# Four tiles of scores in plain fp32 from 40 rows of q and k, and a reordered start

## The chip, the cores and the metric

The kernel runs on one core of a Trainium2 chip. The metric is the device time of one execution in microseconds (us), the median of three timed runs. The core's engines work side by side, each through its own queue in order: TensorE (PE, matrix products), VectorE (DVE), ScalarE (ACT), GpSimd (POOL) and SyncE (SP), which here issues every DMA. An engine that waits for data holds up everything behind it in its queue.

## The reference, cut to what matters

Three parts run one behind another, all in fp32. The first is a gated recurrence (mLSTM) over 2 batches, 8 heads, 768 steps and head size 40:

```python
m_new  = np.maximum(f_gate[t] + m, i_gate[t])
f_stab = np.exp(f_gate[t] + m - m_new); i_stab = np.exp(i_gate[t] - m_new)
C = f_stab * C + i_stab * outer(v[t], k[t])
n = f_stab * n + i_stab * k[t]
y[t] = sigmoid(o_gate[t]) * (C @ q[t]) / max(abs(n @ q[t]), 1)
```

Its output, 1536 tokens of 8*40 = 320 numbers, goes through 4 experts, `relu(x @ w1[e]) @ w2[e]` with 1024 hidden units each, all computed for every token and added with normalized weights. The result goes through a gated feed-forward `((x @ w_a) * (x @ w_b)) @ w_out` with 1536 hidden units.

## The kernel before, in words

The recurrence is computed in chunks of 128 steps. Tile n is chunk n // 2 of batch n % 2, so there are 12 tiles, two to a chunk, and tiles 0 and 1 have no earlier state. A tile's 8 heads are handled in two halves hh of four heads. For each half, `s1a` (L369) makes two products on PE: `pt_a`, the decay exponents, from `LT` and `Rr` (L378), and `pt_c`, the scores, from k and q (L382, four products). ACT takes exp of `pt_a` into `w_t` (L383), POOL zeroes what lies in the future (affine_select, L384), and `s1b` multiplies the scores in on DVE (L389). `s2a` multiplies `w_t` with the values into `pt_y` (L399). `o_gate` makes the output gate (reciprocal on DVE, L417), `s2b` divides and gates (`dn_t`, L434 to L436; `x_t`, L439 and L440), `s3` transposes `x_t` (`pt_x`, L127 to L129) and splits it into a high part `xh` (ACT) and a low part `xl` (DVE).

Precision: an fp32 number is split into two fp32r numbers, hi + lo, which PE multiplies in one pass. For the scores, q and k are loaded three times down 120 rows (`qk_t`, 480 KB for four heads, L274), copied to fp32r by ACT (L284) and turned into low parts in two of the three row groups by two DVE subtractions (L287), so that one product over 120 rows gives hi*hi + lo*hi + hi*lo. The first NF = 2 tiles skip this: their 120 rows hold q and k once with zeros in k below, and the product runs in plain fp32, which PE does in two passes (the trace shows 8 records for four heads instead of 4).

`Rr[b]` (one for each batch) has constant rows 64 to 111, copied from `rsel` once (L498, L499, on ACT), and rows 0 to 63 built anew for each chunk from the gates' cumulative sums (`build_R`, L367). For chunk 0 DVE builds `Rr[0]` in two halves and POOL builds `Rr[1]`. The gates of a chunk run as a chain on DVE with two copies on ACT: `mr`, `lf`, `cm`, `L`, `zh`, `zx`, `LT` (`gate1` to `gate3`, L310 to L337).

The weights of an expert half ("block", 0 to 7) come in 8 pieces through a ring of RB = 3 buffers `raw` (L81). A piece is loaded, copied to its high half `wh` by ACT (L83), and the low half `wl` is subtracted on DVE or POOL (L85), which frees the buffer. The string `LOENG[block]` says which engine: "v" DVE, "p" POOL, and in block 2 all "v". While the recurrence runs, blocks 0 to 2 are already applied: a stream of hidden slices of 128 units for 256 tokens, with eight products `psa` (L196), `hh` on ACT (L213), `hl` on DVE (L214), and products into `psy` (L236 to L238). Blocks 3 to 13 follow in phase 2, which needs nothing from the recurrence but x.

Loads go through SP in order. A `qk_t` load needs one of QB = 3 buffers free, and each DMA uses one of eight completion semaphores in turn, so that it is issued only once the DMA eight places ahead has landed.

The order on each engine isn't the order of the code. A scheduler simulates a timeline and lines the instructions up as it expects them to become ready, so a change in one place moves instructions in others.

Of the kernel before, what the change touches and what calls it, by code (L numbers as in the profile page):

```python
# [33 lines left out]
NF = 2  # L34
LOENG = {0: "pvpvpvpv", 1: "ppvppvpp", 2: "vvvvvvvv", 3: "vpvpvpvp", 4: "vpvpvpvp", 5: "vpvpvpvp"}
LAG = (1, 2)
RB = 3
BS = 4
QB = 3
# [9 lines left out]
def mlstm_moe_kernel(ctx, tc, gates, qk, qc, kvo, dp, w1b, w2b, ident_d, bdmask_d, rsel_d, exp_d, out):  # L49
# [7 lines left out]

    # ---------------------------------------------------------------- constants
    ident = const.tile([P, P], F32, name="ident")
# [8 lines left out]

    # ---------------------------------------------------------------- weights
    wblk = {}  # L70

    def piece1(i, s, pool, lo_eng):
        """One of NP1 parts of expert block i, in the order in which the hidden slices need them:
        fp32 = hi + lo, both exact in fp32r."""
        if s == 0:
            wblk[i] = (pool.tile([P, WB1], F32R, tag="wh", name=f"wh{i}"), pool.tile([P, WB1], F32R, tag="wl", name=f"wl{i}"))
        wh, wl = wblk[i]
        st = WB1 // NP1
        cs = slice(s * st, (s + 1) * st)
        raw = rawp.tile([P, st], F32, tag="raw", name=f"raw{i}_{s}")  # L80
        nc.sync.dma_start(raw, w1b[i][:, cs])  # L81
        yield
        nc.scalar.copy(wh[:, cs], raw)  # L83
        yield
        lo_eng.tensor_tensor(wl[:, cs], raw, wh[:, cs].bitcast(F32), op=ALU.subtract)  # L85

    def piece2(i, s, pool):
        """One of NP2 parts of a float64 block: its bits -> fp32 top (21 significant bits, sign and
        exponent; 0 below fp32's range) and the low word scaled behind it; hi + lo carries 24 bits
        and more."""  # L90
        if s == 0:
# [26 lines left out]
    def split_x(ps, c, o):  # L118
        """The three transposed blocks in ps -> hi and lo parts at columns o of chunk c."""
        hv = xh[c][:, :, o:o + P]  # L120
        nc.scalar.copy(hv, ps)
        nc.vector.tensor_tensor(xl[c][:, :, o:o + P], ps[:, 0:2, :], xh[c][:, 0:2, o:o + P].bitcast(F32), op=ALU.subtract)
        r = xh[c][64:128, 2, o:o + P]
        nc.vector.tensor_tensor(r, ps[64:128, 2, :], r.bitcast(F32), op=ALU.subtract)
# [5 lines left out]

    # ---------------------------------------------------------------- background work
    class Back:
        """Work cut into short steps, handed out between the matrix products."""

# [18 lines left out]
    def lagged(gens):  # L153
        """Runs the first step of each generator one generator ahead."""
        gens = list(gens)
        next(gens[0])
        yield
        for i, g in enumerate(gens):
            if i + 1 < len(gens):
                next(gens[i + 1])  # L160
            for _ in g:
                yield
            yield
# [3 lines left out]

    # ---------------------------------------------------------------- expert steps
    class Stream:
        """A feed-forward stream: step A of an item runs one item ahead of its step B."""  # L170

# [26 lines left out]
    class Item:  # L198
        """One 128-row slice of the hidden layer for n tokens at column o of chunk c."""

# [47 lines left out]

    # ================================================================ phase 1
    stream = Stream()  # L250
    with ExitStack() as c1:
# [18 lines left out]
        def load_qk(n, hh):  # L270
            """Four heads of q and k, three times down the rows."""
            t = td.setdefault(n, {})
            t["qk", hh] = a2.tile([KS, 2, 512], F32, tag="qk", name="qk_t", bufs=QB)
            nc.sync.dma_start(t["qk", hh].rearrange("p a b -> p (a b)"), qk[n, hh])  # L274

        def split_qk(n, hh, engs=QENG):
            """q_hi k_hi + q_lo k_hi + q_hi k_lo as one product over KS rows. (The first tiles' rows
            are q k once and zeros, and they go as fp32 while the tensor engine has time.)"""
            if n < NF:
                return  # L280
# [9 lines left out]
        def load_kvo(n):  # L290
            t = td.setdefault(n, {})
            t["kvo"] = a2.tile([P, NK + NV + DM], F32, tag="kvo", name="kvo_t", bufs=3)
            nc.sync.dma_start(t["kvo"], kvo[n])
            if n >= 2:
                t["qc"] = a2.tile([120, 3 * P], F32, tag="qc", name="qc_t", bufs=2)
                nc.sync.dma_start(t["qc"], qc[n])
# [74 lines left out]
        def s1a(n, hh):  # L371
            """Exponents and scores of four heads."""
            j, b = n // 2, n % 2
            t = td[n]
            t["w", hh] = w = a2.tile([P, 512], F32, tag="w", name="w_t", bufs=3)
            qs = t["qk" if n < NF else "qs", hh]
            pa = ps_t.tile([P, 512], F32, tag="t", name="pt_a")
            nc.tensor.matmul(pa, LT[j % 2], Rr[b][:, 4 * hh:4 * hh + 4, :].rearrange("p h t -> p (h t)"), start=True, stop=True)  # L378
            pc = ps_t.tile([P, 512], F32, tag="t", name="pt_c")
            for h in range(4):  # L380
                hs = slice(h * P, (h + 1) * P)
                nc.tensor.matmul(pc[:, hs], qs[:, 1, hs], qs[:, 0, hs], start=True, stop=True, skip_group_check=True)  # L382
            nc.scalar.activation(w, pa, AF.Exp)  # L383
# [7 lines left out]
        def s2a(n, hh):  # L391
            """Values of four heads; with the last four, what the state of earlier chunks gives."""
            j, b = n // 2, n % 2
# [14 lines left out]
        def o_gate(n):  # L408
            """1 / (1 + exp(-o))."""
            kv = td[n]["kvo"]  # L410
# [66 lines left out]

        # ---------------- start
        nc.gpsimd.memset(rmask, 1.0)
# [10 lines left out]
        for t in LT:  # L490
            nc.vector.memset(t[0:64].bitcast(F32), 1.0)
        load_qk(0, 0)
        load_kvo(0)
        load_qk(0, 1)
        load_qk(1, 0)
        nc.sync.dma_start(ident, ident_d)
        load_kvo(1)
        nc.scalar.copy(Rr[0][64:G], rsel[64:G, 0:H].unsqueeze(2).to_broadcast([48, H, P]))  # L498
        nc.scalar.copy(Rr[1][64:G], rsel[64:G, H:2 * H].unsqueeze(2).to_broadcast([48, H, P]))  # L499
        gate1(0, nc.vector)  # L500
        gate2(0)
        gate3(0)
        build_R(0, nc.vector, 0, 4)
        build_R(0, nc.vector, 4, 8)
        build_R(1, nc.gpsimd)
        gate4(0)
# [8 lines left out]
        s2a(0, 1)  # L515
        load_qk(1, 1)
        s1a(1, 0)
# [36 lines left out]
        def after(key, n, fn, *args):  # L554
            """Keeps work that could run ahead behind an instruction of tile n on its engine."""
            i = td.get(n, {}).get(key)
            with tc.issue_after(i) if i is not None else ExitStack():
                fn(*args)
# [38 lines left out]

    # ================================================================ phase 2
    wp1 = ctx.enter_context(tc.tile_pool(name="wp1", bufs=1, reuse_waits="tile"))
# [152 lines left out]
```

## Time and profile before

| | |
|---|---|
| timed runs | 687.88, 687.70, 686.26 us; median 687.7 |
| profiled execution, first to last instruction | 687.3 us (the only time that its profile gives) |
| PE busy | 641.4 us, 93% of the span |
| DVE busy | 442.9 us, 64% |
| ACT, POOL busy | 264.7 us (39%), 197.1 us (29%) |
| loaded | 45.97 MB, 70 GB/s over the span |

The span is 0.4 us under the median. PE is the engine that works nearly all the time, so what shortens the run is mostly idle time of PE, or time in which it runs at half clock, that goes away. Both are densest in the first 75 us. [...]

### The profile page before, as it was taken

Reading aid. Unit: us, or ns where it says so; the run is one execution under the profiler, and the core shown is the slowest. Engines: PE = TensorE matmul, PEld = TensorE weight load, DVE = VectorE, ACT = ScalarE, POOL = GpSimd, SP = SyncE. Lnnn points to the kernel's source line nnn. Section 1 sums busy time; section 2 is a strip of 40 time slices with the busy share of each in tenths; the row PEclk is TensorE's granted clock in tenths of the full one; section 3 lists DMA queues with packets and bytes.
Section 4 is the critical chain, followed back from the end, with each engine's and each line's share of the span. In section 5 each row is a group of like instructions: output and inputs, shape, how many; then the busy total and the mean of one; then the engine's idle time right before and its main releaser. Section 6 shows DMA issues by size and latency. Waiting matters only on the chain.

```text
span 687.3 us, 10380 instructions
## 1 busy us (share of the span) xinstructions
PE 641.4 (93%) x3831; PEld 584.0 (85%) x3831; DVE 442.9 (64%) x868; ACT 264.7 (39%) x595; POOL 197.1 (29%) x218
## 2 busy tenths in 40 slices
PE   7596999798997999999999999799989999999997
PEld 7586999798996889998888888788868888888886
DVE  5989897989889632233494783954976743434343
ACT  5454635353355453131352442532554322222221
POOL 3457343534136333040160340610433400000000
PEclk9598999899999999999999999989999999999999
DMA  8795652243044352010040130310121000000012
GB/s 233 195 268 166 162 156 68 82 120 87 2 129 119 93 137 74 0 53 1 1 114 17 50 81 1 90 41 1 50 82 33 1 0 1 1 1 0 1 39 77
DMA packets 26247, 48.61 MB, mean 71 GB/s; under 512 B 3101, under 2 KB 15637, under 8 KB 26197
## 3 DMA queue, kind: packets, MB, share of 16 engines
q1 hardware_dynamic: 26197, 47.95, 25.5%
q8 instruction: 30, 0.49, 0.3%
q14 instruction: 20, 0.16, 0.1%
HBM read 45.97 MB, written 1.97 MB: 70 GB/s over the span
## 4 chain that ended last, share of the span: by engine, by line
PE 61%; DVE 20%; DMA 6%; issue 6%; POOL 3%; ACT 3%; DVEq 0%; SPq 0%; POOLq 0%; ACTq 0%
PE psa L196 24%; PE psb L196 9%; PE psy L238 8%; PE psy L236 8%; PE psy L237 7%; DMA raw<-in_w1b 3%; DVE tp L115 3%; DVE tp L107 2%; DVE tp L106 2%; DVE hl L214 2%; DVE acc L247 2%; PE pt_y L399 2%; DVE tp L109 1%; DMA qk_t<-in_qk 1%; PE pt_c L382 1%
## 5 line engine op out<-in xcount | busy, mean ns | idle before, releaser
L236 PE MATMUL psy<-wh,hh 128*128 128x320 f32 x528 | 165.1, 318 | 11.9 <-DVE acc L247 6.1
L237 PE MATMUL psy<-wl,hh 128*128 128x320 f32 x528 | 162.2, 311 | 0.0
L238 PE MATMUL psy<-wh,hl 128*128 128x320 f32 x528 | 142.6, 317 | 10.9 <-DVE hl L214 9.9
L214 DVE SCALAR_TENSOR_TENSOR hl<-psa,hh 128x256 fp32r<-128x256 f32 (+1 forms) x132 | 70.6, 537 | 101.5 <-ACT hh L213 101.3
L196 PE MATMUL psa<-xh,wh 128*128 128x512 f32 (+1 forms) x504 | 123.2, 351 | 1.5 <-DVE hl L214 1.5
L196 PE MATMUL psa<-xh,wl 128*128 128x512 f32 (+1 forms) x504 | 123.2, 350 | 0.0
L236 PEld LDWEIGHTS psy<-wh,hh 128*128 128x128 f32 x528 | 100.4, 190 | 18.3 <-ACT hh L213 7.9
L213 ACT ACTIVATE hh<-psa 128x256 fp32r<-128x256 f32 (+1 forms) x132 | 62.7, 478 | 131.1 <-PE psa L196 131.1
L238 PEld LDWEIGHTS psy<-wh,hl 128*128 128x128 f32 x528 | 93.5, 190 | 15.7 <-DVE hl L214 13.5
L237 PEld LDWEIGHTS psy<-wl,hh 128*128 128x128 f32 x528 | 100.6, 190 | 3.3
L196 PEld LDWEIGHTS psa<-xh,wh 128*128 128x128 f32 x504 | 87.6, 193 | 12.5 <-DVE hl L214 1.9
L196 PEld LDWEIGHTS psa<-xh,wl 128*128 128x128 f32 x504 | 86.0, 191 | 11.5
L196 PE MATMUL psa<-xl,wh 128*128 128x512 f32 (+1 forms) x336 | 91.6, 347 | 0.0
L116 POOL TENSOR_TENSOR wl<-tp,lf 128x272 fp32r<-128x272 f32 x48 | 43.3, 914 | 133.4 <-DVE tp L115 133.1
L223 DVE TENSOR_TENSOR g<-psa,bs 128x512 f32<-128x512 f32 x36 | 24.8, 690 | 78.5 <-PE psa L196 77.3
L196 PEld LDWEIGHTS psa<-xl,wh 128*128 128x128 f32 x336 | 59.2, 191 | 7.6
L85 POOL TENSOR_TENSOR wl<-raw,wh 128x352 fp32r<-128x352 f32 x38 | 39.1, 1035 | 73.5 <-ACT wh L83 73.4
L113 POOL TENSOR_TENSOR lf<-lf,sq 128x272 f32<-128x272 f32 x48 | 46.6, 977 | 41.9 <-DVE sq L110 37.8
L224 ACT CAST hh<-g 128x512 fp32r<-128x512 f32 x36 | 22.4, 621 | 58.0 <-DVE g L223 58.0
L219 ACT COPY bs<-psb 128x512 f32<-128x512 f32 x36 | 21.1, 587 | 60.7 <-PE psb L196 60.7
L83 ACT CAST wh<-raw 128x352 fp32r<-128x352 f32 x64 | 30.1, 487 | 32.4 <-DMA raw<-in_w1b 29.6
L247 DVE SCALAR_TENSOR_TENSOR acc<-psy,pg,acc 128x320 f32<-128x320 f32 x72 | 35.2, 541 | 7.2 <-PE psy L238 7.2
(116 smaller groups left out, 902.7 us busy)
## 6 DMA issues: line engine op xcount, KB each, us to landing
raw<-in_w2b SPq DMA_DIRECT2D x48, 272.0 KB, 2.8
qk_t<-in_qk SPq DMA_DIRECT2D x24, 480.0 KB, 4.9
raw<-in_w1b SPq DMA_DIRECT2D x64, 176.0 KB, 2.5
kvo_t<-in_kvo SPq DMA_DIRECT2D x12, 524.5 KB, 5.5
out<-acc SPq DMA_DIRECT2D x12, 160.0 KB, 2.0
qc_t<-in_qc SPq DMA_DIRECT2D x10, 180.0 KB, 2.9
gt<-in_gates SPq DMA_DIRECT2D x6, 112.0 KB, 4.1
bdmask<-in_bdmask_d SPq DMA_DIRECT2D x1, 173.0 KB, 4.3
```

Source lines behind the costliest of these rows:

```text
L83: nc.scalar.copy(wh[:, cs], raw)
L85: lo_eng.tensor_tensor(wl[:, cs], raw, wh[:, cs].bitcast(F32), op=ALU.subtract)
L113: nc.gpsimd.tensor_tensor(lf, lf, sq, op=ALU.mult)
L116: nc.gpsimd.tensor_tensor(wl[:, cs], tf, lf, op=ALU.add)
L196: nc.tensor.matmul(ps, l, r, start=(i == 0), stop=(i == len(prs) - 1))
L213: nc.scalar.activation(self.hh, ps, AF.Relu)
L214: nc.vector.scalar_tensor_tensor(self.hl, ps, 0.0, self.hh.bitcast(F32), op0=ALU.max, op1=ALU.subtract)
L223: nc.vector.tensor_tensor(g, ps, bs, op=ALU.mult)
L236: nc.tensor.matmul(ps, lh, wh[:, off:off + DM], start=(fi == 0), stop=False)
L237: nc.tensor.matmul(ps, lh, wl[:, off:off + DM], start=False, stop=False)
L238: nc.tensor.matmul(ps, ll, wh[:, off:off + DM], start=False, stop=(fi == nf - 1))
L247: nc.vector.scalar_tensor_tensor(acc[n][:, :DM], ps, pg[:, n, e:e + 1], acc[n][:, :DM], op0=ALU.mult, op1=ALU.add)
```

## The change

Constants, loads and scores, cut to the core (comments that were removed are left out):

```diff
+NP = 4
-LOENG = {0: "pvpvpvpv", 1: "ppvppvpp", 2: "vvvvvvvv", 3: "vpvpvpvp", 4: "vpvpvpvp", 5: "vpvpvpvp"}
+LOENG = {0: "pppppppp", 1: "ppvppvpp", 2: "vvvvvvvv", 3: "vpvpvpvp", 4: "vpvpvpvp", 5: "vpvpvpvp"}
...
         def load_qk(n, hh):
...
-            t["qk", hh] = a2.tile([KS, 2, 512], F32, tag="qk", name="qk_t", bufs=QB)
-            nc.sync.dma_start(t["qk", hh].rearrange("p a b -> p (a b)"), qk[n, hh])
+            tag, bufs = ("qs", 2) if (n, hh) == (1, 1) else ("qk", QB)
+            t["qk", hh] = a2.tile([KS, 2, 512], F32, tag=tag, name="qk_t", bufs=bufs)
+            v = t["qk", hh].rearrange("p a b -> p (a b)")
+            for r0, r1 in ((0, 32), (32, D)) if n < NP else ((0, KS),):
+                nc.sync.dma_start(v[r0:r1], qk[n, hh, r0:r1])
 
         def split_qk(n, hh, engs=QENG):
...
-            if n < NF:
+            if n < NP:
                 return
...
             t["kvo"] = a2.tile([P, NK + NV + DM], F32, tag="kvo", name="kvo_t", bufs=3)
+            if n < 2:
+                nc.sync.dma_start(t["kvo"][:, NK:], kvo[n, :, NK:])
+                return
...
-            qs = t["qk" if n < NF else "qs", hh]
+            qs = t["qk" if n < NP else "qs", hh]
+            ks = D if n < NP else KS
...
-                nc.tensor.matmul(pc[:, hs], qs[:, 1, hs], qs[:, 0, hs], start=True, stop=True, skip_group_check=True)
+                nc.tensor.matmul(pc[:, hs], qs[0:ks, 1, hs], qs[0:ks, 0, hs], start=True, stop=True, skip_group_check=True)
```

The start:

```diff
         load_qk(0, 0)
+        load_qk(0, 1)
         load_kvo(0)
-        load_qk(0, 1)
         load_qk(1, 0)
+        load_qk(1, 1)
+        load_kvo(1)
         nc.sync.dma_start(ident, ident_d)
-        load_kvo(1)
-        nc.scalar.copy(Rr[0][64:G], rsel[64:G, 0:H].unsqueeze(2).to_broadcast([48, H, P]))
-        nc.scalar.copy(Rr[1][64:G], rsel[64:G, H:2 * H].unsqueeze(2).to_broadcast([48, H, P]))
+        for b in range(B):
+            nc.gpsimd.tensor_copy(Rr[b][64:G], rsel[64:G, b * H:(b + 1) * H].unsqueeze(2).to_broadcast([48, H, P]))
...
-        build_R(0, nc.vector, 0, 4)
-        build_R(0, nc.vector, 4, 8)
-        build_R(1, nc.gpsimd)
+        for b in range(B):
+            build_R(b, nc.vector, 0, 4)
+            build_R(b, nc.vector, 4, 8)
...
-        load_qk(1, 1)
+        for n in range(2):
+            nc.sync.dma_start(td[n]["kvo"][:, 0:NK], kvo[n, :, 0:NK])
```

Tiles 0 to 3 load 40 rows (160 KB, as 32 and 8 rows) instead of 120 (480 KB), and tiles 2 and 3 are no longer split but scored in plain fp32. The second half of tile 1 gets a buffer of another kind, so its load no longer waits for one. Tiles 0 and 1 load v and the gate first (344 KB) and the k that the state needs (180 KB) behind the first weights. All low halves of block 0 go to POOL.

The scheduler lines the whole of phase 1 up anew; phase 2 keeps its order. Three places follow, before and then now. (Line numbers move: by 1 for the weights, by 7 or 8 from the gates on.)

The first is DVE, between the weights of tile 0 (`w_t`, two multiplications) and that of tile 1, first half; before:

```order
L389 TENSOR_TENSOR w_t<-pt_c,w_t 128x512 x2
L417 RECIPROCAL r_t<-r_t 128x320
L434 TENSOR_SCALAR dn_t<-pt_y 128x8
L389 TENSOR_TENSOR w_t<-pt_c,w_t 128x512
L310 SCALAR_TENSOR_TENSOR mr<-gt,mr 112x128
L435 TENSOR_TENSOR dn_t<-pt_y,dn_t 128x8
```

Now, on the same engine from the reciprocal on:

```order
L425 RECIPROCAL r_t<-r_t 128x320
L317 SCALAR_TENSOR_TENSOR mr<-gt,mr 112x128
L559 TENSOR_REDUCE psm<-dpt 128x12
L320 TENSOR_TENSOR lf<-gt,mr 112x128
L322 TENSOR_TENSOR cm<-gt,mr 48x128
L560 TENSOR_SCALAR psm<-psm 128x12
L321 TENSOR_TENSOR lf<-lf,mr 112x128
L561 RECIPROCAL psm<-psm 128x12
L328 TENSOR_SCALAR lf<-lf 112x128
L562 TENSOR_TENSOR pg<-dpt,psm 128x48
L332 SCALAR_TENSOR_TENSOR L<-rmask,lf 112x128
L397 TENSOR_TENSOR w_t<-pt_c,w_t 128x512
```

The gates of chunk 1 (`mr` to `L`) and the experts' normalization (`psm`, `pg`) now stand ahead of tile 1's first weights.

The second is POOL, around the four selections of tiles 0 and 1 (`w_t`) and the `Rr` of chunk 1; before:

```order
L367 TENSOR_TENSOR Rr_114<-zx,rsel 64x1024
L384 AFFINE_SELECT w_t<-w_t 128x512 x3
L85 TENSOR_TENSOR wl_232<-raw_0_233,wh_231 128x352
L85 TENSOR_TENSOR wl_232<-raw_2_237,wh_231 128x352
L384 AFFINE_SELECT w_t<-w_t 128x512
```

Now, from the third selection to the fourth and on (`wl_239` is the low half of block 0, `raw_3` its fourth piece, `eb` a small gate product):

```order
L392 AFFINE_SELECT w_t<-w_t 128x512
L86 TENSOR_TENSOR wl_239<-raw_3_382,wh_238 128x352
L356 TENSOR_TENSOR eb<-expd,ex 16x2
L86 TENSOR_TENSOR wl_239<-raw_4_386,wh_238 128x352
L374 TENSOR_TENSOR Rr_113<-zx,rsel 64x1024
L86 TENSOR_TENSOR wl_239<-raw_5_390,wh_238 128x352
L374 TENSOR_TENSOR Rr_114<-zx,rsel 64x1024
L392 AFFINE_SELECT w_t<-w_t 128x512
L86 TENSOR_TENSOR wl_239<-raw_6_394,wh_238 128x352
L86 TENSOR_TENSOR wl_239<-raw_7_398,wh_238 128x352
```

The fourth selection, which tile 1's second half needs, now stands behind both `Rr` of the next chunk and three low halves.

The third is DVE up to the first `hl` of the stream of hidden slices (`wl_232` is block 0); before:

```order
L85 TENSOR_TENSOR wl_232<-raw_3_375,wh_231 128x352
L85 TENSOR_TENSOR wl_232<-raw_5_383,wh_231 128x352
L122 TENSOR_TENSOR xl_75<-pt_x,xh_72 128x2x128
L124 TENSOR_TENSOR xh_72<-pt_x,xh_72 64x128
L389 TENSOR_TENSOR w_t<-pt_c,w_t 128x512
L287 TENSOR_TENSOR qs_t<-qk_t,qs_t 40x512 x2
L389 TENSOR_TENSOR w_t<-pt_c,w_t 128x512
L417 RECIPROCAL r_t<-r_t 128x320
L287 TENSOR_TENSOR qs_t<-qk_t,qs_t 40x512 x2
L85 TENSOR_TENSOR wl_232<-raw_7_391,wh_231 128x352
L464 TENSOR_TENSOR cbd_t<-pt_u,bdmask 120x369
L214 SCALAR_TENSOR_TENSOR hl<-psa,hh 128x256
```

Now, the twelve rows that end with the same `hl` (`wl_655` is block 2; two rows ahead of these stands the last `x_t` multiplication of tile 1, behind a low half of block 1):

```order
L397 TENSOR_TENSOR w_t<-pt_c,w_t 128x512
L123 TENSOR_TENSOR xl_75<-pt_x,xh_72 128x2x128
L125 TENSOR_TENSOR xh_72<-pt_x,xh_72 64x128
L86 TENSOR_TENSOR wl_655<-raw_0_656,wh_654 128x352
L397 TENSOR_TENSOR w_t<-pt_c,w_t 128x512
L425 RECIPROCAL r_t<-r_t 128x320
L86 TENSOR_TENSOR wl_655<-raw_1_658,wh_654 128x352
L86 TENSOR_TENSOR wl_655<-raw_2_713,wh_654 128x352
L472 TENSOR_TENSOR cbd_t<-pt_u,bdmask 120x369
L86 TENSOR_TENSOR wl_655<-raw_3_717,wh_654 128x352
L472 TENSOR_TENSOR cbd_t<-pt_u,bdmask 120x369
L215 SCALAR_TENSOR_TENSOR hl<-psa,hh 128x256
```

The eight subtractions `qs_t` of tiles 2 and 3 are gone from DVE. The first `hl` now stands behind the fourth piece of block 2, which is the 20th piece of weights; before it stood behind the 8th. On ACT the first `hh` likewise stands behind the copy of the 20th piece and behind the first `qs_t` copy of tile 4.

## Rows read from the trace of the kernel before

**Rows 1.** Waits of PE, 0 to 90 us: total us, times, longest us.

```profile
PE psy L236 <- ACT hh L213: 4.5, 3, 2.5
PE pt_x L127 <- DVE x_t L440: 4.3, 1, 4.3
PE pt_c L382 <- DMA qk_t<-in_qk: 3.5, 1, 3.5
PE psy L238 <- DVE hl L214: 3.1, 1, 3.1
```

**Rows 2.** Stages: us; busy PE, PEld, DVE, ACT, POOL; PE clock; DMA share; GB/s.

```profile
31.00:42.00 11.00, 9.53 (x54) 8.72 (x52) 10.82 (x15) 6.27 (x14) 3.95 (x5) 0.71 0.75 192
55.00:66.00 11.00, 5.39 (x41) 4.88 (x39) 10.84 (x19) 4.16 (x12) 9.22 (x8) 0.94 0.68 205
66.00:74.00 8.00, 8.00 (x43) 7.79 (x43) 6.76 (x15) 3.53 (x11) 0.86 (x2) 0.66 0.55 143
74.00:98.00 24.00, 23.85 (x192) 23.44 (x191) 23.05 (x46) 13.26 (x30) 10.16 (x12) 1.00 0.57 158
```

**Rows 3.** Timeline of PE: start us, us, instruction, [idle before, releaser].

```profile
11.95 1.77 PE L382 MATMUL pt_c<-qk_t 120*128 120x128 f32 x8
...
30.73 0.45 PE L127 MATMUL pt_x<-ident,x_t 128*128 128x128 f32 x1 [4.29 <-DVE x_t L440]
...
33.43 1.10 PE L382 MATMUL pt_c<-qs_t 120*128 120x128 f32 x4
...
35.61 1.16 PE L196 MATMUL psa<-xh,wh 128*128 128x256 f32 x4
...
41.95 0.41 PE L236 MATMUL psy<-wh,hh 128*128 128x320 f32 x1 [1.47 <-ACT hh L213]
...
45.02 0.54 PE L238 MATMUL psy<-wh,hl 128*128 128x320 f32 x2
...
66.59 0.84 PE L196 MATMUL psa<-xh,wh 128*128 128x256 f32 x3
```

**Rows 4.** Timeline of DVE.

```profile
6.81 1.93 DVE L337 SCALAR_TENSOR_TENSOR LT<-zh,rsel,cm 48x128 fp32r<-48x128 f32 x1 [0.19 <-ACT zh L329]
...
14.43 2.14 DVE L417 RECIPROCAL r_t<-r_t 128x320 f32<-128x320 f32 x1
...
17.31 0.96 DVE L310 TENSOR_TENSOR_SCAN mr<-gt,mr 112x128 f32<-112x128 f32 x1
...
21.17 0.41 DVE L325 TENSOR_TENSOR_SCAN L<-rmask,lf 112x128 f32<-112x128 f32 x1
...
26.28 0.35 DVE L337 SCALAR_TENSOR_TENSOR LT<-zh,rsel,cm 48x128 fp32r<-48x128 f32 x1
...
28.67 1.92 DVE L440 TENSOR_TENSOR x_t<-x_t,r_t 128x320 f32<-128x320 f32 x1
30.62 3.46 DVE L287 TENSOR_TENSOR qs_t<-qk_t,qs_t 40x512 fp32r<-40x512 f32 x4
...
62.07 2.91 DVE L85 TENSOR_TENSOR wl<-raw,wh 128x352 fp32r<-128x352 f32 x2
```

**Rows 5.** Timeline of POOL.

```profile
6.71 1.89 POOL L367 TENSOR_TENSOR Rr<-zx,rsel 64x1024 fp32r<-64x1024 f32 x1 [5.54 <-DVE zx L336]
10.78 0.64 POOL L384 TENSOR_SCALAR_AFFINE_SELECT w_t<-w_t 128x512 f32<-128x512 f32 x1 [2.19 <-ACT w_t L383]
...
26.32 3.91 POOL L367 TENSOR_TENSOR Rr<-zx,rsel 64x1024 fp32r<-64x1024 f32 x2 [0.22 <-DVE zx L336]
30.49 0.93 POOL L85 TENSOR_TENSOR wl<-raw,wh 128x352 fp32r<-128x352 f32 x1 [0.25 <-ACT wh L83]
```

**Rows 6.** The page: the weights' copies on ACT, their loads (us to landing).

```profile
L83 ACT CAST wh<-raw 128x352 fp32r<-128x352 f32 x64 | 30.1, 487 | 32.4 <-DMA raw<-in_w1b 29.6
...
raw<-in_w1b SPq DMA_DIRECT2D x64, 176.0 KB, 2.5
```

**Rows 7.** DMA issues, 0 to 80 us: KB each, median us to landing.

```profile
raw<-in_w1b SPq DMA_DIRECT2D x25, 176.0 KB, 5.1
```

## The prediction

> **What bounds the kernel now.** The page comes first: PE is busy 93% of the span, so I look for time in which it isn't, or runs slowly. The waits of PE [rows 1] show it: in the first 90 us PE waits 4.5 us for ACT's `hh` (1.5 at 41.95 [rows 3], 2.5 once, so 0.5 for the third), 4.3 for the last `x_t` of tile 1, 3.5 for the load of q and k of tile 1's second half, and 3.1 for `hl`. The busy table by stage [rows 2] says who is behind them: DVE is busy 10.82 of 11 us at 31 to 42 and 10.84 of 11 at 55 to 66, while PE has 5.39 of 11 in the latter. [...] From 74 to 98 us PE is busy 23.85 of 24 us at full clock: from there on a microsecond won earlier is a microsecond at the end, and one lost earlier is not made up. So I follow the change by four places on PE's timeline [rows 3]: the first scores, the transpose `pt_x` of tile 1 at 30.73, the first `hl` product at 45.02 and the seventh group of `psa` at 66.59.
>
> The timelines of DVE and POOL [rows 4, 5] show one thing more. `LT` took 1.93 us at 6.81 and 0.35 at 26.28; the long one lies inside POOL's `Rr` of 6.71 to 8.60 and ends with it. `x_t` at 28.67 took 1.92 and ends with the `Rr` pair of 26.32 to 30.23. [...]
>
> **What the change takes away.** The wait of 3.5 us for q and k goes: the load stands in the first ten now and asks for no buffer that is in use. DVE loses eight `qs_t` subtractions (four took 3.46 us [rows 4]: about 7) and four low halves of block 0 (about 0.5 each where not blocked), and gets two `Rr` halves of 0.65: some 7.5 us less. ACT loses four `qs_t` copies and two constants, which cost nothing, since it mostly waits. DMA carries 2.6 MB less (eight loads, 320 KB each). All that would shorten the start if DVE's work alone set it. But the queues are in order, and what now stands ahead of the waiting instruction decides.
>
> **First scores.** POOL copies two constants of 48 x 1024 when `rsel` has landed (3.6 us), just as DVE's gate chain starts. The trace has no such copy. From below, a selection of 512 took 0.64, so 1.28 for 1024; from above, an `Rr` of 1024 with two inputs took 1.89 [rows 5]. I take 1.3, since a copy has one input like the selection. Both copies then hold up the chain, 2.6 us, and what `LT` loses now (1.93 - 0.35 = 1.6) goes: +1.0. The ends are -1.6 (no blocking) and +2.2 (1.89 each). The eight additional issues on SP (about 0.45 each) don't decide: everything tile 0 needs is issued by 4.5 us.
>
> [...]
>
> **Transpose of tile 1.** Second `w_t`: before it ended at 14.43, now at 15.4. Then the reciprocal (2.1), then the gates of chunk 1, which now stand ahead of tile 1's first `w_t`. From `mr` to `L` they took 17.31 to 21.58 [rows 4] with work of tile 0 between; alone I take 3.0. Then `w_t` 0.6, `cm` and `zx` 0.7, and one block by a low half on POOL, 0.9: `zx` is ready at 22.7. POOL's fourth selection now stands behind `Rr` 1.95, a low half 0.93, `Rr` 1.95 and takes 0.64 [rows 5]: 28.2. DVE: `w_t` 0.7, reciprocal 2.1, division about 1.1: 32.1. The last `x_t` then stands behind the low half of block 1's third piece. The buffer for it is free when POOL has done the eighth piece (28.2 + 2 x 0.93 = 30.1); load 2.5, copy 0.49 [rows 6], low half 0.5, `x_t` 0.5: 34.1 against 30.73, **+3.4**. The ends are -1.6 (no blocking, the piece already there) and +6.0 (a load takes the 5.1 us that it took in this stretch before [rows 7]); I take 2.5 since 2.6 MB are gone. So the 3.5 us of the load are not gained: PE meets the same delay one chain later.
>
> **First `hl`.** Scores of four heads in plain fp32 at half clock took 1.77 us, in fp32r 1.10 [rows 3]; two of them lie before the first `psa`: +1.3, so `psa` moves from 35.61 to 40.3. At full clock the other two cost less, about 0.4 each. The first `hh` and `hl` stand behind the 20th piece of weights instead of the 8th. Three buffers: load 2.5, copy 0.49, low half 0.93, issue 0.3, so 4.2 / 3 = 1.4 us a piece; twelve pieces after 30.1 end at 46.9, and `hl` at 47.3. PE's own work comes out at about the same time (40.3, plus the 9.4 of before, less the wait of 1.5 for `hh`, less 1.1 of products that now stand behind). Against 45.02: **+2.5**. Ends: 0 (1.2 us a piece) and +6 (1.7).
>
> **To the seventh group.** From 45.02 to 66.59 PE waited 0.5 + 2.5 + 3.1 = 6.1 us. Now few low halves are left there. But the third `hl` stands behind a `w_t` and a reciprocal (2.8, of which PE covers 1.0: 1.8), and the sixth behind `LT` and four `qs_t` that come after `zx`, while POOL builds two `Rr`: 3.9 + 0.35 + 2.8 + 0.4 = 7.4, of which PE covers 3.0: 4.4. That is 6.2 for 6.1, and 0.3 for fp32: **+2.8** in all. The half clock after it, 0.66 of 8 us, is paid again. Ends: -3 (only one of the two waits is left) and +3.
>
> **After that** PE is dense until 98 us. DVE enters with some five low halves less, which buys nothing where PE is the bound. Sum: 687.3 + 2.8 = 690.1 in the profiled execution's own span; the median of the runs lies 0.4 above it: **690.5 us**.
>
> **Rivals.**
> - *The freed work counts* (faster). Copies on POOL don't collide, the pieces are there in time, and with DVE relieved the waits of 55 to 66 (2.5 + 3.1) go. For it: DVE's 10.84 of 11 us there and `wl` at 62.07, two in 2.91 us, blocked. Against: the places in the queues above. Price: -0.3 at `psa` (-1.6 + 1.3), +0.3 for later fp32, -5.6 for the waits, and half of the clock's 2.7 (0.34 x 8): -7.0 at best; with the block by `Rr` left in the sixth `hl` (2 to 3) -4.5: 683.2. It decides if `pt_x` of tile 1 comes before 31 us. Chance 0.30.
> - *Even* (within 2 us). The start is late as forecast, the stretch to the seventh group shorter by as much (2.8, less than the wait of 3.1 that it has now): 687.7. Chance 0.24.
> - *The ring of weights sets everything* (slower). If loads still take 5.1 us, a piece costs 6.8 / 3 = 2.3 and the 20th piece comes 10.8 us later than I take it; some 4 of that beyond the forecast would remain, as pieces are then ready ahead of later stretches: 694.5. Against: less traffic. Chance 0.08.
> - *It doesn't do what it says*: q and k of tile 1 come late all the same, since each DMA waits for the eighth before it. The 14th load would have to stand; by the issue times it is out by 7 us. Chance 0.01; it ends near the forecast.
>
> The forecast itself has 0.37. A measurement of this kernel can tell about 0.3%, 2.1 us, from no change. Slower by more: forecast, ring and misfit, 0.46; within: 0.24; faster: 0.30. Range: 683.0 to 694.5, which takes in the first rival's own time and the ring's; 688.5 to 693 is the forecast's own (the transpose's and the ring's ends, halved).
>
> **What would show it.** In the changed profile: DVE's gate chain at 3.5 to 9 us with single instructions of over 1 us beside POOL's copies (otherwise the first term is wrong); no wait of PE for `qk_t`; POOL's fourth selection at about 28 us and `pt_x` of tile 1 after 33 (if before 31, the faster rival holds); the first `hl` product at 47 to 48 with a wait for `hh` or `hl` before it; waits for `hl` of together 5 to 7 us until the seventh group. The prediction is wrong if these waits are gone, or if the pieces of weights come faster than one in 1.2 us.

## The result: 1.2% slower, and the profile after

The changed kernel takes 697.05 us (median of 8 runs, 693.48 to 705.72), the kernel before 688.18 (8 runs, 686.26 to 692.51). The run of 705.72 counts as a slow one and is left out of the ratio. The ratio is 1.0122, with a 95% interval of 1.0094 to 1.015: slower by 8.4 us, where the prediction said 2.8 and its range ended at 694.5 us. The profiled execution spans 693.0 us against 687.3, so it shows 5.7 of the 8.4. The executions of the changed kernel differ more among themselves, from a span of 691.8 us at a mean granted clock of 0.962 to 699.5 at 0.953; the middle ones span 695.2 and 695.5, at 0.952 and 0.957, where the profiled one has 0.961. So part of what those lose more than the profiled one is probably half clock; where, is in no profile.

PE's timeline of the changed kernel, to be read beside [rows 3] (start in us from the span's start; duration in us of the group; engine, line, operation; output and inputs; shapes; count; in brackets the idle time ahead and what ended it):

```profile
9.64 1.21 PE L390 MATMUL pt_c<-qk_t 40*128 40x128 f32 x8
15.95 2.07 PE L390 MATMUL pt_c<-qk_t 40*128 40x128 f32 x8
...
32.95 0.44 PE L128 MATMUL pt_x<-ident,x_t 128*128 128x128 f32 x1 [2.15 <-DVE x_t L448]
...
35.71 2.07 PE L390 MATMUL pt_c<-qk_t 40*128 40x128 f32 x8
...
40.55 1.22 PE L197 MATMUL psa<-xh,wh 128*128 128x256 f32 x4
...
45.65 1.16 PE L390 MATMUL pt_c<-qk_t 40*128 40x128 f32 x8
...
49.19 0.54 PE L239 MATMUL psy<-wh,hl 128*128 128x320 f32 x2
...
75.83 0.90 PE L239 MATMUL psy<-wh,hl 128*128 128x320 f32 x2 [5.43 <-DVE hl L215]
76.53 0.84 PE L197 MATMUL psa<-xh,wh 128*128 128x256 f32 x3
```

The wait for q and k is gone. The first scores come 0.4 us earlier (`pt_a` at 9.24 instead of 9.61), `pt_x` of tile 1 2.2 later, the first `psa` 4.9 later, the first `hl` product 4.2 later, the seventh `psa` 9.9 later. That last place overstates the delay: the transpose of tile 3 and `pt_a` of tile 4 (67.79 to 70.40 us) now stand ahead of the seventh `psa`, and stood behind it before. Four heads of plain scores take 2.07 us at a granted clock of 0.50, where fp32r took 1.10, and 1.16 at full clock (1.00), where fp32r took 0.56. PE's table by stage, of the kernel before and then of the changed one (stretch, length, PE's busy time and instructions, granted clock, DMA share, GB/s):

```profile
9.00:44.00 35.00, 25.16 (x142) 0.71 0.90 240
44.00:100.00 56.00, 49.60 (x369) 0.94 0.63 176
```

```profile
9.00:44.00 35.00, 29.27 (x117) 0.52 0.71 188
44.00:100.00 56.00, 48.38 (x358) 0.93 0.50 138
```

Up to 44 us PE is busy 4.1 us longer with fewer products, at a mean clock of 0.52 instead of 0.71. So I keep three accounts for each kernel, from its busy table in slices of 2 us: PE's idle time; what half clock costs (busy time times one minus the granted clock); and the rest, PE's work at full clock. They add up to the span:

| profiled execution | span | idle | half clock | work |
|---|---|---|---|---|
| before | 687.3 | 45.9 | 17.9 | 623.5 |
| changed | 693.0 | 42.0 | 21.8 | 629.2 |
| after_np2 (below) | 689.3 | 41.6 | 21.6 | 626.1 |
| after_np2_r_back | 686.3 | 38.9 | 22.6 | 624.8 |
| after_scores23_twice | 696.0 | 41.6 | 22.3 | 632.1 |
| after_warm100 | 693.9 | 43.6 | 18.2 | 632.2 |
| before_np4 | 696.3 | 45.8 | 23.2 | 627.3 |

The change did win 3.9 us of PE's idle time. It gave 3.9 back to half clock and 5.7 to work. The account of work isn't exact: kernels with the same products on PE as the changed one have 627.1 (after_r_back, below) and 627.7 (after_lo_dve), so it is known to some 2 us.

### The profile page after: what moved, and what is told of

Its sections match the earlier page's. It is cut to its first block, busy times and chain, and to the rows that moved or that the text cites. A ratio compares the mean times of both kernels' runs of the same rounds, so it can differ in the third digit from the quotient of the medians.

```text
span 693.0 us, 10399 instructions
## 1 busy us (share of the span) xinstructions
PE 651.1 (94%) x3847; PEld 587.4 (85%) x3847; DVE 435.8 (63%) x858; ACT 260.0 (38%) x589; POOL 194.6 (28%) x223
## 4 chain that ended last, share of the span: by engine, by line
PE 63%; DVE 23%; issue 5%; DMA 5%; ACT 2%; POOL 2%; SPq 0%; DVEq 0%; POOLq 0%; ACTq 0%
PE psa L197 25%; PE psb L197 8%; PE psy L239 8%; PE psy L237 8%; PE psy L238 7%; DVE tp L116 3%; DVE tp L108 2%; DMA raw<-in_w1b 2%; PE pt_y L407 2%; DVE qs_t L291 2%; DVE tp L107 2%; DVE tp L110 2%; PE pt_c L390 2%; DVE hl L215 2%; DVE acc L248 2%
## 5 line engine op out<-in xcount | busy, mean ns | idle before, releaser
L225 ACT CAST hh<-g 128x512 fp32r<-128x512 f32 x36 | 22.3, 621 | 58.4 <-DVE g L224 58.4
```

## The experiments

All ran in five rounds beside the kernel before; ratios are to it. Those called pinned edit single instructions of the finished program, so that every engine keeps its order exactly; in the others the scheduler lines phase 1 up anew.

### One part undone, one part alone

**after_np2**: tiles 2 and 3 go as fp32r again.

```diff
-NP = 4
+NP = 2
```

> The changed kernel with tiles 2 and 3 split into high and low parts and scored in fp32r over 120 rows as before; only tiles 0 and 1 stay plain over 40 rows. DVE gets eight subtractions back (about 7 us), ACT four copies, DMA 1.3 MB. If the plain scores of tiles 2 and 3 carry the loss (2.07 us each at half clock before the first psa, and all of the split work bunched at tile 4): 3 to 5 us faster than the changed kernel. Rival (DVE's relief is worth more than the slower scores): 1 to 4 us slower.

Measured 1.0037 (1.0013 to 1.006), that is 0.85% or 5.9 us faster than the changed kernel. The plain scores of tiles 2 and 3 carry most of the loss, and the seven us that they free on DVE don't make up for it. The two profiled executions differ by 3.7 us, of which 3.1 are work.

**before_np4**: the mirror, in the kernel before.

```diff
+NP = 4
-            if n < NF:
+            if n < NP:
-            qs = t["qk" if n < NF else "qs", hh]
+            qs = t["qk" if n < NP else "qs", hh]
+            ks = D if n < NP else KS
-                nc.tensor.matmul(pc[:, hs], qs[:, 1, hs], qs[:, 0, hs], ...)
+                nc.tensor.matmul(pc[:, hs], qs[0:ks, 1, hs], qs[0:ks, 0, hs], ...)
```

> The kernel before with one part of the change alone: tiles 2 and 3 scored plainly, and all four tiles over 40 rows (loads as before). If the loss sits in this part: 4 to 7 us slower than before. Rival (it costs only together with the early loads and R): within 2 us of before.

Measured 1.0155 (1.0136 to 1.0174): slower by 10.7 us from this part alone, more than expected and more than from the whole change. Idle time is the same as before (45.8), though DVE has less to do; work (+3.8) and half clock (+5.3) are the loss. The order is another one too: `pt_x` of tile 1 comes at 33.92 instead of 30.73, so not all of the 10.7 us need be the price of the plain scores themselves.

**after_r_back**: the first `Rr` as before.

```diff
-        for b in range(B):
-            nc.gpsimd.tensor_copy(Rr[b][64:G], ...)
+        nc.scalar.copy(Rr[0][64:G], ...)
+        nc.scalar.copy(Rr[1][64:G], ...)
-        for b in range(B):
-            build_R(b, nc.vector, 0, 4)
-            build_R(b, nc.vector, 4, 8)
+        build_R(0, nc.vector, 0, 4)
+        build_R(0, nc.vector, 4, 8)
+        build_R(1, nc.gpsimd)
```

> The changed kernel with the constants of R copied by ACT and R of the second batch row built on POOL, as before. By the prediction's first step (POOL's copies hold up DVE's gate chain) the first scores come about as before, 9.2 to 9.6 us, since what the copies cost LT gets back; the time stays within 1.5 us of the changed kernel (695.5 to 698.5). Rival (R on DVE and the copies on POOL carry the loss): 3 to 6 us faster than the changed kernel.

Measured 1.0076 (1.0058 to 1.0094), 3.2 us faster than the changed kernel: the rival's lower end. What differs is the order on POOL and on DVE. POOL's queue, in the changed kernel and then with this part undone:

```profile
21.21 1.94 POOL L374 TENSOR_TENSOR Rr<-zx,rsel 64x1024 fp32r<-64x1024 f32 x1
...
24.01 2.13 POOL L374 TENSOR_TENSOR Rr<-zx,rsel 64x1024 fp32r<-64x1024 f32 x1
26.10 0.63 POOL L392 TENSOR_SCALAR_AFFINE_SELECT w_t<-w_t 128x512 f32<-128x512 f32 x1
```

```profile
20.38 0.63 POOL L392 TENSOR_SCALAR_AFFINE_SELECT w_t<-w_t 128x512 f32<-128x512 f32 x1 [3.47 <-ACT w_t L391]
...
28.06 3.99 POOL L374 TENSOR_TENSOR Rr<-zx,rsel 64x1024 fp32r<-64x1024 f32 x2 [1.00 <-PE pt_x L130]
```

The fourth selection stands ahead of both `Rr` again, and on DVE the `w_t` that needs it stands ahead of `xl` and `xh` of tile 0 (22.34 instead of 28.06). `pt_x` of tile 1 comes at 30.44, 2.5 earlier than in the changed kernel, and the first `psa` at 35.91, 4.6 earlier, in part because one group of scores now stands behind it.

**after_np2_r_back**: both of these diffs together. 

> The changed kernel with two parts undone together, the plain scores of tiles 2 and 3 and the place of R and its constants; what is left of the change is the loads of 40 rows for tiles 0 and 1, their early place, and the low halves on POOL. If the two losses add up (0.85% and 0.46% of the changed kernel's 1.2%): 0.997 to 1.001 of before. If both cure the same delay (PE late at the first psa): 1.002 to 1.005 of before.

Measured 1.0012 (0.9999 to 1.0025), between the two ranges and next to the first: the two nearly add up (1.10 of 1.31%), and what is left of the change (early loads of 40 rows, low halves on POOL) is worth nothing measurable, though PE idles 7.0 us less than before.

**after_lo_dve**: four low halves of block 0 on DVE again.

```diff
-LOENG = {0: "pppppppp", ...}
+LOENG = {0: "pvpvpvpv", ...}
```

> The changed kernel with the low halves of block 0 dealt out as before, every second one on DVE. By the prediction's steps the fourth selection is freed by 0.9 us and a piece of weights costs less, so psa and the first hl come 1 to 2 us earlier; the sixth hl still waits behind LT and qs_t, so 1 to 2 us faster than the changed kernel in all. Rival (DVE's relief counts after all): DVE has 2 us more to do and the kernel is 1 to 2 us slower. If the low halves have no part in the loss: within 1 us.

Measured 1.0189 (1.0164 to 1.0214), 4.6 us slower than the changed kernel, outside all that was expected; DVE's timeline says why:

```profile
15.07 0.97 DVE L86 TENSOR_TENSOR wl<-raw,wh 128x352 fp32r<-128x352 f32 x1 [4.12 <-ACT wh L84]
15.97 1.28 DVE L397 TENSOR_TENSOR w_t<-pt_c,w_t 128x512 f32<-128x512 f32 x2
```

The scheduler put a low half ahead of the very first `w_t`, and DVE stood 4.1 us for ACT's copy of its piece; `w_t` came at 15.97 instead of 11.43. This is a price of that order, not of the low half's 0.5 us. **before_lo_pool** has the same diff reversed, in the kernel before. 

> The kernel before with one part of the change alone: all low halves of block 0 on POOL. By the prediction's steps (a low half on POOL holds up the selections of tile 1 and the ring of raw buffers) 0 to 2 us slower than before. Rival (DVE's relief counts: the low halves on DVE stand ahead of w_t and wait for loads there): 2 to 4 us faster than before.

Measured 1.0016 (0.9999 to 1.0032): no difference.

### PE's work in the plain scores

**after_scores23_twice** (pinned): each plain product of tiles 2 and 3 is issued a second time.

```diff
+    new = {i.name: i.__replace__(name=..., sync_info=<waits only>) for i in SCORES23}
+    blk.instructions = [x for i in blk.instructions for x in ([new[i.name], i] if i.name in new else [i])]
```

> The changed kernel with the sixteen plain score products of tiles 2 and 3 each issued twice (same inputs, same output), nothing else moved: the price of these products doubled. In the changed kernel's profile they take 2.07 us for four heads at half clock (two groups) and 1.16 at full (two groups), 6.5 us in all, where fp32r took 3.1. If PE's own work there is the loss of the four plain tiles: 5 to 7 us slower than the changed kernel, and half of that is what plain scores cost against fp32r. Rival (the loss comes from what the missing splits do to the order on DVE and ACT; PE has room there): 0 to 2 us slower.

Measured 1.0162 (1.0143 to 1.018), 2.8 us slower than the changed kernel, between the two. The products themselves grew by 1.71 us a group at half clock and 0.89 at full:

```profile
35.97 3.78 PE L393 MATMUL pt_c<-qk_t 40*128 40x128 f32 x16
...
49.49 2.05 PE L393 MATMUL pt_c<-qk_t 40*128 40x128 f32 x16
```

Four groups together grew by 5.2 us, and the first `hl` product came 4.7 later (53.90); the waits for `hl` behind it swallowed some. Work grew by 2.9, and the end of the profiled execution moved by 3.0: of the 5.2 us of added products, more than half is paid at the end.

### The clock

**before_rows40** (pinned): in the kernel before, the scores of tiles 0 and 1 run over 40 rows; loads unchanged.

```diff
+                if n < NF:
+                    SWAPS.append((i, D, (64, 128)))
...
+        kw = dict(ins=tuple(rows(p, r) for p in i.ins), tile_size=t)
+        new[i.name] = i.__replace__(**kw)
```

> The kernel before, with one thing changed and every instruction in its old place: the scores of tiles 0 and 1 are products over 40 rows instead of 120 (the 80 rows left out are zeros on the k side, so the result is the same; the loads stay whole). Clock theory: with products over 40 rows the clock that falls at about 10.7 us does not come back at about 14 us; score products of four heads at 14.7 and 20 us take 2.07 us instead of 1.05, the granted clock at 12 to 16 us is 0.50 instead of 0.82. The time moves by 0 to +2 us, since PE waits 3.5 us for q and k of tile 1's second half at about 20 us anyway. Rival (the longer gap ahead of the first scores lost the clock, 3.1 us instead of 2.1): rows don't matter, clock and time are those of before. No change of time in either theory beyond 0.3%.

Measured 1.0035 (1.002 to 1.005), that is 2.4 us slower, a little more than expected. The stage of 12 to 20 us, before and then with 40 rows (columns as above):

```profile
12.00:16.00 4.00, 4.00 (x31) 0.82 1.03 334
16.00:20.00 4.00, 0.86 (x7) 1.00 0.99 258
```

```profile
12.00:16.00 4.00, 4.00 (x18) 0.52 1.02 330
16.00:20.00 4.00, 3.56 (x15) 0.50 1.01 262
```

PE is as busy as before at 12 to 16 us, and the granted clock is 0.52 there and 0.50 behind it, where in the kernel before it was 1.00 by 14.

**after_load120_rows40** and **after_load120_rows120** (pinned): the changed kernel with whole loads for tiles 0 and 1, products over 40 and over 120 rows.

```diff
+                if n < NF and r0 == 32:
+                    SWAPS.append((i, KS - 32, None))
```

The second runs the products likewise, with `(i, KS, (128, 128))`.

> The changed kernel with the four loads of q and k of tiles 0 and 1 whole again (120 rows, 1.3 MB more in the first 10 us), every instruction in its place, products still over 40 rows. It is the control for the next kernel. Both theories: clock at half from 10.8 to 44 us as in the changed kernel, time 0 to +3 us of the changed kernel, by what the loads come later.

> As the control, and the score products of tiles 0 and 1 run over 120 rows (80 of them zeros on the k side). [...] Rival (queues): the clock comes back, but the w_t of tile 1 waits for POOL's selection behind its Rr all the same, and the time stays within 1 us of the control. Rival (gap): the clock does not come back.

Measured 1.0218 (1.0197 to 1.024) and 1.0187 (1.0162 to 1.0211): the heavier loads cost 6.6 us, more than expected, since all that SP issues behind them comes later: DVE stands 5.0 us for the gates of chunk 1, and `mr` comes at 22.04 instead of 16.36. With 120 rows `pt_y` at 18 us takes 1.02 us instead of 2.00. The difference of 2.1 us lies within the intervals.

**after_rows40_fulltile** (pinned): the 40 rows issued as products for the whole array instead of half of it.

```diff
+                if n < NP:
+                    SWAPS.append((i, D, (128, 128)))
```

> The changed kernel with one field changed in the finished order: the plain products over 40 rows of tiles 0 to 3 are issued for the whole array (128 rows by 128 columns) instead of for half of it (64 by 128), the rows of data stay 40. If the clock follows the part of the array that a product claims: it is back at full at 14 to 15 us and the kernel is 2 to 4 us faster than the changed kernel. If it follows the rows that carry data: clock at half from 10.8 to 44 us as in the changed kernel, time within 1 us of it.

Measured 1.0138 (1.0113 to 1.0164): no difference. As in the changed kernel, the groups took what they take at half clock: `pt_c` 1.91 us each at 11.59, 15.43 and 19.27 and `pt_y` 1.84 at 13.29, 17.13 and 20.97, where a `pt_c` over 40 rows took 1.16 at full clock (45.65 us in the changed kernel).

**after_warm100** (pinned): 35 more products over zeros ahead of the first scores.

```diff
+    more = [w.__replace__(name=f"I-{900000 + k}") for k in range(35)]
...
+            ins[at.index(w.name):at.index(w.name)] = more
```

> The changed kernel with 35 more of the bf16 products over zeros that PE runs before the first scores (100 instead of 65), so that PE's idle time of 3.1 us ahead of the first scores is filled. If the gap is what costs the clock at 10.8 us: full clock until 20 us or longer, 3 to 6 us faster than the changed kernel. If the clock falls all the same once the scores over 40 rows run: within 1.5 us of the changed kernel, the fall perhaps 1 to 3 us later.

Measured 1.0121 (1.0099 to 1.0142). Here the clock's fall follows the gap (`pt_y` took 1.12 us at 14.82 and 2.00 behind the wait of 1.69), and the time does not care:

```profile
1.06 8.55 PE L498 MATMUL pt_w<-wz 128*128 128x128 bf16 x100 [1.06 <-DVE wz L495]
...
13.74 1.16 PE L393 MATMUL pt_c<-qk_t 40*128 40x128 f32 x8
...
18.99 2.00 PE L410 MATMUL pt_y<-kvo_t,w_t 128*128 128x82 f32 x8 [1.69 <-DVE w_t L400]
...
33.03 0.45 PE L131 MATMUL pt_x<-ident,x_t 128*128 128x128 f32 x1 [2.16 <-DVE x_t L451]
...
40.64 1.22 PE L200 MATMUL psa<-xh,wh 128*128 128x256 f32 x4
```

The scores run at full clock to 17 us (1.16 us for each of the four groups), PE then waits for DVE, and `pt_x` and `psa` come within 0.1 us of where they came without. Half clock before 33 us costs nothing that can be told in this kernel. **after_np2_r_back_warm100** does the same to the kernel with two parts undone. 

> The kernel with two parts undone (plain scores of tiles 2 and 3, place of R) and the same 35 more products. If the gap costs the clock: 2 to 4 us faster than without them, 0.995 to 0.998 of before, so faster than both kernels. If the scores over 40 rows cost it: within 1 us.

Measured 1.0007 (0.9988 to 1.0025), and **after_np2_r_back_rows120**, which clears the four buffers of tiles 0 and 1 and scores over 120 rows there:

```diff
+            if n < 2:
+                (nc.vector if hh == 0 else nc.gpsimd).memset(t["qk", hh], 0.0)
...
-            ks = D if n < NP else KS
+            ks = D if 2 <= n < NP else KS
```

> As the kernel before it in this list, and the first four buffers of q and k are set to zero ahead of the loads (two by DVE, two by POOL), so that the scores of tiles 0 and 1 run over 120 rows, 80 of them zeros, without the loads of 120 rows. Clock theory: full clock at 14 to 20 us, 2 to 3 us faster than the kernel before it in this list. Rival (PE isn't the bound there once the two parts are undone): within 1 us.

This one measured 1.0005 (0.999 to 1.002): neither differs from 1.0012 or from before.

**before_np4_rows120** and **after_rows120_tiles23** (pinned): 120 rows for all plain scores in before_np4, and for tiles 2 and 3 in the changed kernel (with whole loads, as in after_load120). The first has

```diff
+                if n < NP:
+                    SWAPS.append((i, KS, (128, 128)))
```

and the second the same for `2 <= n < NP`.

> The kernel before with tiles 2 and 3 scored plainly, as in the run of that part alone, and with every instruction in the same place as there; only the plain score products of tiles 0 to 3 run over 120 rows (80 of them zeros on the k side) instead of 40. If the clock that stays at half behind pt_x of tile 1, where PE is dense, carries a good part of that run's loss of 10.7 us: the clock is at full from 38 us or earlier instead of from 44, the first scores of the fourth group take 1.05 us, and the time falls by 3 to 5 us (1.008 to 1.011 of before). If it is the order behind the missing splits and PE's doubled work alone: within 1 us (1.014 to 1.017).

> The changed kernel with q and k of tiles 2 and 3 loaded whole (1.3 MB more at 17 to 24 us) and their plain scores over 120 rows (80 of them zeros on the k side), nothing moved; tiles 0 and 1 stay as they are. Clock theory for the dense stretch: full clock from 38 to 40 us instead of from 44, 2 to 4 us faster than the changed kernel (1.006 to 1.009 of before). Rival (clock there is worth nothing, as the first hl waits for ACT's copy of tile 4's load at 47 us): within 1.5 us of it.

Measured 1.0122 (1.0087 to 1.0157) and 1.0186 (1.0161 to 1.0211). The first gives 2.3 us back, between the two expectations and with intervals that overlap; the second loses 4.4, since its heavier loads delay `pt_x` of tile 1 to 37.34. The profile of the first shows what can keep a better clock from paying. It is of the slowest of the six executions, 703.2 us against 694.7 to 696.5, so the others may differ. PE's stages, without and with 120 rows:

```profile
40.00:44.00 4.00, 4.00 (x20) 0.50 0.94 235
44.00:48.00 4.00, 4.00 (x26) 0.80 0.97 274
48.00:52.00 4.00, 4.00 (x35) 1.00 1.01 343
```

```profile
40.00:44.00 4.00, 3.98 (x33) 0.98 0.87 231
44.00:48.00 4.00, 1.34 (x10) 0.88 1.01 303
48.00:52.00 4.00, 3.97 (x17) 0.50 0.97 283
```

PE is done sooner, stands for 2.7 us, and falls back to half clock. For 2.0 of them it waits for ACT's first `hh` (ACT with 120 rows):

```profile
46.65 1.04 ACT L288 CAST qs_t<-qk_t 120x1024 fp32r<-120x1024 f32 x1 [2.23 <-DMA qk_t<-in_qk]
47.60 0.38 ACT L217 ACTIVATE hh<-psa 128x256 fp32r<-128x256 f32 x1
```

The copy of tile 4's first load stands ahead of the first `hh`. That load needs a buffer that the plain scores of tile 2 read, and these free it when PE is done with them, in the changed kernel at 40.62; before, DVE's subtraction freed it at 34.08. In the changed kernel SP issues the load at 41.36, behind the 18th to 20th piece of weights, and the copy starts at 46.75. Before, SP issued it at 34.16, and the copy, at 42.27, stood behind the first `hh`. What SP waited for in the changed kernel from 38 to 42 us (us in total, times, longest):

```profile
SPq L82 <- POOL wl L86: 1.5, 1, 1.5
SPq L278 <- PE pt_c L390: 0.3, 1, 0.3
```

The 0.3 us are those of a load of tile 3, at 37.81; the load of tile 4 found its buffer free when SP came to it. With 120 rows the scores end at 39.12 and SP comes to the load at 41.90, so there the weights ahead of it hold it longer than the buffer, and a fourth buffer alone would not have brought it sooner in this order.

### The wait for the sixth hl

**after_hl_first** (pinned): `hl` moved ahead of the four `qs_t` that took 6.58 us.

```diff
+    hl = ins.pop(at.index("I-733"))
+    ins.insert(order.index("I-899"), hl)
```

> The changed kernel with one instruction moved in the finished order: the sixth hl stands ahead of the four qs_t of tile 4 on DVE instead of behind them; nothing else moves. Blocking theory: PE no longer waits 5.4 us for it (the four took 6.58 us beside POOL), nor runs the next 2.5 us at half clock: 3 to 6 us faster than the changed kernel. Rival (PE only comes sooner to the next thing that these four hold up, the scores of tile 4 and the next hl): within 1.5 us of the changed kernel.

Measured 1.0109 (1.0081 to 1.0138): 0.9 us faster than the changed kernel, which can't be told from no difference. PE's next stop takes over:

```profile
67.59 0.56 PE L239 MATMUL psy<-wh,hl 128*128 128x320 f32 x2 [1.49 <-DVE hl L215]
71.38 0.46 PE L239 MATMUL psy<-wh,hl 128*128 128x320 f32 x2
77.39 0.63 PE L390 MATMUL pt_c<-qs_t 120*128 120x128 f32 x4 [4.01 <-DVE xh L125]
```

The scores of tile 4 wait for `xh`, which stands on DVE behind the same four `qs_t`. **after_split_early** let these four start behind `x_t` of tile 2.

```diff
-                ... after, "last", n0 - LAG[0], split_qk, n0, 0), ...
+                ... after, "last", n0 - (2 if j == 2 else LAG[0]), split_qk, n0, 0), ...
```

> The changed kernel, but the split of tile 4's first two loads (two copies on ACT, four subtractions qs_t on DVE) may start behind x_t of tile 2 instead of tile 3, so that it stands ahead of POOL's Rr of tiles 4 and 5. In the changed kernel these four took 6.58 us beside POOL and the sixth hl waited behind them (PE idle 5.4 us). Blocking theory: the four take 2.8 us, the wait at the sixth hl goes to under 2 us, and the half clock behind it goes too: 3 to 5 us faster than the changed kernel. Rival (the wait is only moved, since PE is then held by the next chain): within 1 us.

Measured 1.0154 (1.012 to 1.0188). The four took 3.19 us, and PE's longest wait for `hl` fell from 5.43 to 2.33, yet the kernel is not faster. Since the scheduler moved the start too (`psa` at 41.83 instead of 40.55), its time tells nothing on the wait.

No kernel here is faster than the one before.

## Why the prediction was wrong

The direction was right, and so were the places to look at on PE's timeline. The size failed in what PE itself has to do between them, and two of the agreements on the way are luck.

- *First scores* (+1.0 forecast): -0.4. The collision is there: beside POOL's two copies (2.11 us from 3.64 on) `lf` and `cm` took 0.94 and 1.01 us, as the next rows show, and 0.29 each in the kernel before. But a copy takes 1.05 us, not the 1.3 that I took, and the two cost the chain 1.4 us, while `LT` gave back 1.6 (0.35 instead of 1.93).

```profile
3.91 0.94 DVE L320 TENSOR_TENSOR lf<-gt,mr 112x128 f32<-112x128 f32 x1
4.88 1.01 DVE L322 TENSOR_TENSOR cm<-gt,mr 48x128 f32<-48x128 f32 x1
...
8.03 0.35 DVE L344 SCALAR_TENSOR_TENSOR LT<-zh,rsel,cm 48x128 fp32r<-48x128 f32 x1 [0.18 <-ACT zh L336]
```

- *Transpose of tile 1* (+3.4): +2.2. The fourth selection stood behind both `Rr`, as forecast, but was done at 26.7 instead of 28.2. It wasn't the last wait of the `w_t` that needs it: on DVE that stands behind `xl` and `xh` of tile 0, which wait for ACT's `xh`, a wait that I did not have. So the division ends at 31.97, where I had 32.1, by luck. The low half ahead of the last `x_t` then waited for no load, which gave 1.2 us back.

```profile
27.30 0.42 DVE L123 TENSOR_TENSOR xl<-pt_x,xh 128x256 fp32r<-128x256 f32 x1 [2.91 <-ACT xh L122]
...
28.06 0.69 DVE L397 TENSOR_TENSOR w_t<-pt_c,w_t 128x512 f32<-128x512 f32 x1
...
31.89 0.52 DVE L86 TENSOR_TENSOR wl<-raw,wh 128x352 fp32r<-128x352 f32 x1
```

  The gain of 3.5 us at the load was indeed lost one chain later, and with this order undone the kernel is 3.2 us faster (after_r_back).
- *First `psa`* (+4.7): +4.9, by luck too. From `pt_x` to `psa` PE took 7.6 us, where I had 6.2, and `pt_x` came 1.2 sooner than forecast. *First `hl`* (+2.5): +4.2. From `psa` on PE took 8.6 us without a wait, where I had 6.8 of its own work; it was at half clock until 44 us. The ring of weights kept its price (the low half of the 20th piece was done at 45.86, forecast 46.9), and ACT's copy of tile 4's load, which I left out, came no sooner (46.75).
- *Waits up to the seventh group* (6.2 us): 0.6 + 1.5 + 5.4 = 7.5. But with the longest of them gone the kernel was no faster that could be told (after_hl_first).
- *The failed step* is the price of the plain scores on PE: the +1.3 ahead of the first `psa`, and "0.3 for fp32" behind it. I had 1.3 for two groups and about 0.4 each for the other two, and then let the waits for `hl` swallow nearly all of the latter. Measured, plain against fp32r is 0.97 us a group at half clock (2.07 - 1.10) and 0.60 at full (1.16 - 0.56), 3.1 in all, and after_scores23_twice shows that more than half of such work comes out at the end. My 1.77 us for a group at half clock was a row in which the clock changed [rows 3]; the kernel before has a group at half clock throughout, 2.05 us at 20.34. The part costs still more: 5.9 us by after_np2, 10.7 by before_np4. What else it does, the runs show without dividing it: over 40 rows the plain scores keep PE at half clock until 44 us in the stretch where it is dense (a granted clock of 0.50 at 40 to 44 us in before_np4, 0.98 over 120 rows), where before full clock came back at 37.4, and they free tile 4's buffer later. Taking back the half clock alone gave 2.3 us, within the noise, and in the execution profiled PE then stood for the load into that buffer (before_np4_rows120).
- The rival *the freed work counts* was half right: idle time did fall by 3.9 us. Half clock and PE's work took more than that.

The rest is open. Of the 5.7 us of additional work the rows of the score groups explain 2.8 (4 x 0.60 for tiles 2 and 3, 4 x 0.11 for the first two tiles, 1.16 against 1.05), and some 2 may be the account's own error. Why the executions of the changed kernel differ by 8 us among themselves is not shown.

## What to carry to other kernels

Where PE is busy 93% of the span, price first what a change adds to PE's own work, at the clock of that stretch and from a row that ran at one clock throughout, and only then the waits that it removes on other engines: here seven microseconds less on DVE did not make up for three more on PE. Price also what frees a buffer after the change: here the next tile's load moved from behind a DVE subtraction to behind a PE product, and then behind pieces of weights in SP's queue. Where a chain comes out as forecast, look which wait ended last all the same: here it was another one. And test a wait by moving the one instruction: a wait of 5.4 us was worth nothing that could be told, since the next product stood behind the same work.

## What the runs showed of the hardware

- In the changed kernel PE's granted clock was 0.50 from 10.8 to 44 us, though PE was busy without a gap from 9.2 to 25 and from 33 on, with scores over 40 rows among its products. With nothing but the rows of the scores of tiles 0 and 1 changed in the kernel before, the clock at 12 to 16 us was 0.82 over 120 rows (1.00 from 14 on) and 0.52 over 40, with 0.50 at 16 to 20 (before_rows40). Where PE came to the 40-row scores at full clock (after_warm100), four groups took 1.16 us each up to 17.3 us; behind a wait of 1.69 us `pt_y` took 2.00, where it had taken 1.12. Rows are not all: the kernel before, over 120 rows, also had 0.50 from 20.3 to 26.4 us, busy without a gap.
- A group of four heads over 40 rows took longer when it was issued for half of the array than for the whole (after_rows40_fulltile): 2.07 us instead of 1.91 at half clock. In the changed kernel the first of its eight records took 0.58 us and the other seven 0.42; the 0.16 us between them is as much as the difference.
- Four `qs_t` on DVE took 2.81 us where POOL was idle (68.03 us in the kernel before) and 6.58 (68.86 us in the changed kernel) beside POOL's `Rr` pair (66.70 to 70.68) and the `kw_t` pair behind it.
